# Eight PSUM tiles of one bank in the place of four of two banks

## The chip, the cores and the metric

The kernel runs on one core of a Trainium2 chip. The metric is the device time of one execution in microseconds, taken as the median of several runs.

TensorE (PE) multiplies and writes PSUM, an accumulator memory that this kernel uses as eight banks of 2 KB in each partition. VectorE (DVE) and ScalarE (ACT) read PSUM; GpSimd (POOL) here works on SBUF only; SyncE (SP) issues most of the DMAs. The engines run side by side, each through its own instructions in order, and wait for one another by semaphores.

## The reference

Attention, a gated projection, and a feed-forward block with layer norm, one after another (batch 4, 448 positions, 12 heads of 64, so 1792 rows of 768):

```python
def _moe_ref(x, w_val, conv_w, w_out):
    ...
    gate = 1.0 / (1.0 + np.exp(-gate_pre))      # gate_pre: causal convolution of x, 5 taps
    val = x @ w_val
    return (gate * val @ w_out).astype(np.float32)

def _moe2_ref(x, g_ln, w_ch1, w_ch2):
    mu = np.mean(x, axis=-1, keepdims=True)
    var = np.mean((x - mu) ** 2, axis=-1, keepdims=True)
    xn = (x - mu) / np.sqrt(var + 1e-06) * g_ln
    ch = np.maximum(xn @ w_ch1, 0.0) @ w_ch2     # 768 -> 3072 -> 768
    return (x + ch).astype(np.float32)

def reference(**kwargs):
    attn_out = _attn_ref(**attn_kwargs)          # causal softmax attention
    x = ...                                      # heads side by side
    x = _moe_ref(x=x, **moe_kwargs)
    return _moe2_ref(x=x, **moe2_kwargs)
```

## The kernel before

The attention and the gate fill the first 254.9 us; the change doesn't touch them. Behind them come three stages of matmuls.

The **w_out stage** (254.9 to 356.9 us). `tile_steps(n)` handles 128 rows, for 14 tiles. TensorE multiplies gate * val by w_out (L812, 36 matmuls of 384 columns), the two halves of the 768 columns into the two banks of one PSUM tile (tag "o": `Z[0]` and `Z[1]` in turn). VectorE takes the statistics of each half (`bn_stats`, L827) and their sums (L835, L836), POOL the power (L839), VectorE the shift (L840). ACT copies the tile for the residual (`ka`, L830) and writes the normalised tile to SBUF (`kn`, L842), in one instruction each for both banks. TensorE transposes it in six blocks (`kt`, L848) into another PSUM tile (tag "x": `Z[3]` and `Z[2]` in turn), and VectorE scales it by g_ln into SBUF (`fx`, L851), again in one instruction. `right_blocks` then makes seven operands of each two tiles: additions (`tt`, L712) and a split of each operand into a high (ACT, L866) and a low part (DVE, L867).

The **W1 stage** (356.9 to 684.7 us), `unit1`. The product with w_ch1 is computed by a scheme of seven block products; each product runs for two groups of rows (512 and 384 columns wide), in six visits of the weights. One unit is one product of one group: nine matmuls (L1038) into one bank, 168 units in all. The sums of products are made partly by accumulating in a bank and partly by emptying it: ACT copies the first results to SBUF (L1050), VectorE adds later ones to the copies (L1053), ACT applies the relu (L1009), and ACT issues the store to DRAM (L1014). Meanwhile ACT and DVE prepare the weights of the coming visits from DRAM (L264 to L283, L751, L753, additions L712), and parts of them are stored by SP (L975).

The **W2 stage** (684.7 to 1001.7 us), `unit`. The same scheme for w_ch2: 196 units of nine matmuls of 384 columns (L1154). VectorE alone empties the banks, by an addition to a sum in SBUF (L1165); ACT and DVE make both operands (L1136, L1137, L1098, L1099).

The eight banks in W1 and W2 are three rings, by the letter that the unit's number in "ACABACA" has (`MINE` in W2):

```python
Z = [ps.tile([P, 2, 512], F32, name=f"z{i}") for i in range(4)]
"A": [Z[3][:, 0], Z[0][:, 0], Z[1][:, 0], Z[2][:, 0]], "C": [Z[3][:, 1], Z[1][:, 1]], "B": [Z[0][:, 1], Z[2][:, 1]],
```

So neighbouring banks of one tile serve different rings. The planner knows banks: `Plan.ready` asks whether the users of the same place of the ring are done. The waits in the program itself are made afterwards by the tile framework, from the tile that an instruction reads or writes (`reuse_waits="tile"` of the pool `ps`).

What sets the order: all of this is handed to `Plan` as steps, `task(cost, fn, due, ...)`, each with an engine (or several), a cost in ns and a due time. `arrange()` goes through time and gives each free engine the ready step with the earliest due time; the instructions of each engine are written in that order. `TUNE` shifts the due times by kind of step, and `HOME` says for some additions whether POOL or VectorE takes them.

Of the kernel before, what the change touches and what calls it, by code (L numbers as in the profile page):

```python
# [52 lines left out]
class Plan:  # L53
# [28 lines left out]
    def task(self, cost, fn, due, after=(), new=(), uses=(), lag=0, mode=None, hog=False, behind=None, key=None):  # L82
        due += self.tune.get(key, 0)
        if key in self.home:
            cost = {self.home[key]: {'POOL': 1040, 'DVE': 554}[self.home[key]]}

        def run():
            for b in new:
                b.tile = self.place(b)
            fn(k.engine)  # L90

        k = Task(cost, run, due, after, new, uses, lag, mode, hog, behind)
        self.tasks.append(k)
        return k
# [91 lines left out]
def attention_gate_ffn(  # L186
# [428 lines left out]
    JJ = 3  # L615
# [12 lines left out]
    with ExitStack() as ph2, tc.manual_schedule():  # L628
# [10 lines left out]
        Z = [ps.tile([P, 2, 512], F32, name=f"z{i}") for i in range(4)]  # L639
# [18 lines left out]
        def raw_view(t):  # L658
# [11 lines left out]
            "o": [Z[0], Z[1]], "x": [flat(Z[i]).rearrange("p (c f) -> p c f", f=P) for i in (3, 2)],  # L670
# [6 lines left out]
            "A": [Z[3][:, 0], Z[0][:, 0], Z[1][:, 0], Z[2][:, 0]], "C": [Z[3][:, 1], Z[1][:, 1]], "B": [Z[0][:, 1], Z[2][:, 1]],  # L677
# [53 lines left out]
        def products_of(who, wa, ws, narrowed, due, out):  # L731
# [7 lines left out]
            k1 = task({"POOL": 1040}, lambda e: tt(e, s(), q(2)(), q(3)(), ALU.add), due + 0.2, narrowed, [ws], [wa], hog=True, key=who + "s1")  # L739
            k3 = task({"POOL": 1040}, lambda e: tt(e, q(2)(), q(0)(), q(2)(), ALU.subtract), due + 0.6, [k1], [], [wa], hog=True, key=who + "s3")  # L740
# [498 lines left out]
```

## Time and profile before

| | us |
| --- | --- |
| median of 3 runs | 1007.7 (1007.18 to 1008.37) |
| profiled execution | 1007.35 |
| its span | 1005.6 |
| TensorE busy | 963.7 |
| VectorE busy | 765.0 |
| ScalarE busy | 561.6 |
| GpSimd busy | 294.5 |
| granted TensorE clock, mean | 0.998 |

The span is the stretch that the profile covers, from the first instruction to the last; 1.75 us of the execution lie outside it. Matmuls overlap one another, so a busy TensorE says little of single stops: these are seen in the chain of waits, which is the row of instructions and releases that ended last, and in the list of what TensorE waited for. In the rows below an instruction reads "line engine operation out<-in", and the names leave the numbers of tiles out: every PSUM tile of these stages is `z`. Where the number matters, the order of the compiled program has it (z0_3198 is `Z[0]`, z3_3201 is `Z[3]`).

### The profile page before, as it was taken

What the parts mean: (1) busy time and instruction counts of PE and PEld (TensorE: products, weight loads), DVE (VectorE), ACT (ScalarE), POOL (GpSimd) and SP (SyncE); (2) the same over time, 40 slices, a digit from 0 to 9 for tenths busy, and PEclk for the clock granted to TensorE, in tenths of its full rate; (3) what the DMA queues carried; (4) which work ended last, traced back from release to release, by engine and by line L of the source; (5) the groups of instructions that cost most, each with busy time, mean ns of one, the idle gap of its engine ahead of it and who ended that gap; (6) DMA issues with size and microseconds to landing.
All of it is one profiled execution on the core that took longest, in us unless ns stands there. A gap on an engine that the chain in (4) does not pass through costs nothing.

```text
span 1005.6 us, 16427 instructions
## 1 busy us (share of the span) xinstructions
PE 963.7 (96%) x5731; PEld 857.0 (85%) x5731; DVE 765.0 (76%) x1549; ACT 561.6 (56%) x1153; POOL 294.5 (29%) x367
## 2 busy tenths in 40 slices
PE   9989999999999989999979999999999999999998
PEld 5657777788999978888868878888999999999998
DVE  6899989864488876666667776667999888979873
ACT  7988878862365556666555556564445335334330
POOL 5888877671032231111111121110110000100100
PEclk9999999999999999999999999999999999999999
DMA  6344445322554467878787877689725424424322
GB/s 199 118 158 146 153 154 164 113 83 87 160 173 143 141 225 249 254 222 264 244 251 250 271 223 237 207 265 321 272 84 179 145 63 157 134 82 147 126 95 95
DMA packets 115474, 177.26 MB, mean 176 GB/s; under 512 B 10432, under 2 KB 87744, under 8 KB 115392
## 3 DMA queue, kind: packets, MB, share of 16 engines
q1 hardware_dynamic: 70704, 154.19, 46.3%
q10 hardware_dynamic: 44688, 22.03, 7.5%
q8 instruction: 45, 0.74, 0.3%
q14 instruction: 37, 0.30, 0.1%
HBM read 118.39 MB, written 57.80 MB: 175 GB/s over the span
## 4 chain that ended last, share of the span: by engine, by line
PE 72%; DVE 14%; POOL 4%; DMA 3%; ACT 3%; issue 3%; SPq 0%; ACTq 0%; DVEq 0%; POOLq 0%
PE z L1154 28%; PE z L1038 24%; PE val L599 5%; PE z L812 5%; PE t L443 2%; PE pv L467 2%; PE s L599 2%; DVE g L485 2%; PE s L372 2%; POOL p L408 2%; DVE p L394 1%; DVE x L867 1%; DVE lf L1053 1%; DMA lf<-in_w_ch 1%; DMA hd<-lf 1%
## 5 line engine op out<-in xcount | busy, mean ns | idle before, releaser
L1038 PE MATMUL z<-x,ar 128*128 128x512 f32 (+1 forms) x1224 | 256.5, 368 | 15.4 <-DVE lf L1053 6.3
L1038 PEld LDWEIGHTS z<-x,ar 128*128 128x128 f32 x1224 | 222.9, 189 | 46.5 <-ACT lf L1050 7.9
L712 POOL TENSOR_TENSOR lf<-lf 128x384 f32<-128x384 f32 x52 | 59.4, 1142 | 332.7 <-DVE lf L712 162.3
L1154 PE MATMUL z<-x,x 128*128 128x384 f32 x684 | 125.4, 335 | 1.8 <-DVE lf L1165 0.8
L1165 DVE TENSOR_TENSOR acc<-z,acc 128x384 f32<-128x384 f32 x168 | 91.6, 552 | 46.6 <-PE z L1154 45.4
L1154 PEld LDWEIGHTS z<-x,x 128*128 128x128 f32 x684 | 118.8, 188 | 3.5 <-issue 1.8
L1136 ACT CAST x<-lf 128x384 fp32r<-128x384 f32 x102 | 51.3, 513 | 87.3 <-PE z L1154 67.2
L812 PE MATMUL z<-wo,ar 128*128 128x384 f32 x504 | 91.2, 337 | 0.4 <-DVE ar L801 0.4
L812 PEld LDWEIGHTS z<-wo,ar 128*128 128x128 f32 x504 | 87.0, 188 | 1.1 <-DVE ar L801 0.9
L1154 PE MATMUL z<-x,ar 128*128 128x384 f32 x468 | 85.4, 334 | 0.4 <-ACT ar L1136 0.4
L408 POOL TENSOR_SCALAR p<-p,r 128x128 f32<-128x128 f32 (+1 forms) x144 | 78.4, 567 | 22.4 <-DVE r L404 21.4
L1154 PEld LDWEIGHTS z<-x,ar 128*128 128x128 f32 x468 | 81.4, 188 | 0.7 <-issue 0.7
L400 ACT ACTIVATE p<-p,negm 128x128 f32<-128x128 f32 (+1 forms) x144 | 71.9, 504 | 12.5 <-DVE negm L394 11.7
L485 DVE SCALAR_TENSOR_TENSOR g<-pv,cw,g 128x444 f32<-128x444 f32 (+1 forms) x96 | 64.7, 674 | 11.0 <-POOL g L476 9.0
L1050 ACT COPY lf<-z 128x512 f32<-128x512 f32 (+1 forms) x72 | 37.6, 535 | 52.7 <-PE z L1038 52.0
L1038 PE MATMUL z<-x,w 128*128 128x512 f32 (+1 forms) x288 | 61.8, 366 | 1.4 <-DVE lf L1053 1.4
L1137 DVE TENSOR_TENSOR x<-lf,x 128x384 fp32r<-128x384 f32 x102 | 59.6, 594 | 3.2 <-DMA af<-wd 1.6
L1009 ACT ACTIVATE lf<-lf 128x512 f32<-128x512 f32 (+1 forms) x72 | 41.6, 577 | 36.4 <-DVE lf L1053 32.8
L1038 PEld LDWEIGHTS z<-x,w 128*128 128x128 f32 x288 | 52.4, 188 | 8.6 <-ACT lf L1009 1.8
L1136 ACT CAST ar<-lf 128x384 fp32r<-128x384 f32 x57 | 28.7, 513 | 52.9 <-PE z L1154 43.6
L1053 DVE TENSOR_TENSOR lf<-z,lf 128x512 f32<-128x512 f32 (+1 forms) x72 | 43.5, 618 | 16.5 <-PE z L1038 15.7
L753 DVE TENSOR_TENSOR ar<-lf,ar 128x384 fp32r<-128x384 f32 x62 | 38.1, 619 | 22.8 <-ACT ar L751 22.2
(152 smaller groups left out, 1855.3 us busy)
## 6 DMA issues: line engine op xcount, KB each, us to landing
lf<-in_w_ch SPq DMA_DIRECT2D x31, 768.0 KB, 5.7
af<-wd SPq DMA_DIRECT2D x28, 576.0 KB, 4.9
lf<-hd SPq DMA_DIRECT2D x19, 768.0 KB, 4.4
raw<-in_qk SPq DMA_DIRECT2D x24, 512.0 KB, 4.6
hd<-lf ACTq DMA_DIRECT2D x48, 256.0 KB, 4.1
af<-in_w_ch SPq DMA_DIRECT2D x15, 768.0 KB, 5.2
wd<-af SPq DMA_DIRECT2D x60, 192.0 KB, 3.2
hd<-lf ACTq DMA_DIRECT2D x48, 192.0 KB, 4.5
```

Of the source, the lines that this page charges most:

```text
L400: nc.scalar.activation(reg, reg, AF.Exp, bias=negm.tile[:, i:i + 1], scale=-1.0, accum_out=ssum.tile[:, i:i + 1])
L408: nc.gpsimd.tensor_scalar(reg, reg, r.tile[:, i:i + 1], 1.0, ALU.mult, ALU.mult)
L485: nc.vector.scalar_tensor_tensor(g.tile[:, d:], pv.tile[:, :S - d], cw[:, c, t:t + 1], g.tile[:, d:], ALU.mult, ALU.add)
L599: nc.tensor.matmul(ps.tile[:, :S], w[:, do, kc * P:(kc + 1) * P], x.tile, start=(kc == 0 and i == 0), stop=(kc == KC - 1 and i == 2),)
L712: ENG[eng].tensor_tensor(o, a, b, op)
L812: nc.tensor.matmul(o.tile[:, nh, :HALF], y.tile[:, kc], wo_t[kc][:, a, nh * HALF:(nh + 1) * HALF], start=(count[nh] == 0), stop=(count[nh] ...
L1038: nc.tensor.matmul(b.tile[:, :width], w.tile[:, a, kc], X[g][p][:, c, kc], start=(m == 0 and fresh), stop=(m == 3 * JJ - 1), skip_group_ch ...
L1053: ka = task({"DVE": 154 + int(1.04 * width)}, lambda e: nc.vector.tensor_tensor(q.tile, b.tile[:, :width], q.tile, ALU.add), t1, [k], [], ...
L1136: k_hi = task({"ACT": 514}, lambda e, src=src, h=h: nc.scalar.copy(h.tile[:, 0], src()), due, [need, k_hi], [h], [buf], key=f"chi{i}")
L1137: k = task({"DVE": 554}, lambda e, src=src, h=h: nc.vector.tensor_tensor(h.tile[:, 1], src(), f32(h.tile[:, 0]), ALU.subtract), due + 1, [ ...
L1154: nc.tensor.matmul(b.tile[:, :HALF], h.tile[:, a, jj], w.tile[:, c, jj], start=(n == 0 and fresh), stop=(n == 3 * JJ - 1), skip_group_chec ...
L1165: k = task({"DVE": 554}, lambda e: nc.vector.tensor_tensor(acc(), b.tile[:, :HALF], acc(), ALU.add), t0 + UNIT + 0.2, [k, acc_ld[u]], [], ...
```

## The change

The four tiles of two banks become eight of one bank. What read or wrote two banks in one instruction (the copy `ka`, the normalising `kn`, the scaling `fx`) is now two instructions, one for each bank, and their costs in the planner are raised, as are those of additions on POOL and of the low parts in W2. `TUNE` and `HOME` have new numbers. In `HOME` es2, Xt3, Xt4, Zt1, Zt2, ws1 and T4 go from POOL to DVE; es4, ws3 and T1 go from DVE to POOL. (X and Z are `right_blocks` of the two groups, ws the additions of a W1 visit, T those of W2's weights, es those of W1's first weights.) In the w_out stage 12 additions L712 go to VectorE, and POOL keeps 2 of 14.

```diff
-TUNE = {'eld': -26.4, 'ea': -8.5, 'eb0': 2.2, ...
-HOME = {'es1': 'DVE', 'es3': 'POOL', 'es2': 'POOL', 'es4': 'DVE', 'Xt1': 'DVE', 'Xt2': 'DVE', 'Xt3': 'POOL', ...
+TUNE = {'eld': -20.7, 'ea': -38.2, 'eb0': 2.2, ...
+HOME = {'es1': 'DVE', 'es3': 'POOL', 'es2': 'DVE', 'es4': 'POOL', 'Xt1': 'DVE', 'Xt2': 'DVE', 'Xt3': 'DVE', ...
...
-            cost = {self.home[key]: {'POOL': 1040, 'DVE': 554}[self.home[key]]}
+            cost = {self.home[key]: {'POOL': 1095, 'DVE': 554}[self.home[key]]}
...
-        Z = [ps.tile([P, 2, 512], F32, name=f"z{i}") for i in range(4)]
+        Z = [[ps.tile([P, 512], F32, name=f"z{i}_{h}") for h in range(2)] for i in range(4)]
...
-            "o": [Z[0], Z[1]], "x": [flat(Z[i]).rearrange("p (c f) -> p c f", f=P) for i in (3, 2)],
+            "o": [Z[0], Z[1]], "x": [Z[3], Z[2]],
...
-            "A": [Z[3][:, 0], Z[0][:, 0], Z[1][:, 0], Z[2][:, 0]], "C": [Z[3][:, 1], Z[1][:, 1]], "B": [Z[0][:, 1], Z[2][:, 1]],
+            "A": [Z[3][0], Z[0][0], Z[1][0], Z[2][0]], "C": [Z[3][1], Z[1][1]], "B": [Z[0][1], Z[2][1]],
...
-            ka = task({"ACT": 800}, lambda e: nc.scalar.copy(stage.tile.rearrange("p (a f) -> p a f", a=2), o.tile[:, :, :HALF]),
+            def kept(e):
+                for nh in range(2):
+                    nc.scalar.copy(stage.tile[:, nh * HALF:(nh + 1) * HALF], o.tile[nh][:, :HALF])
+
+            ka = task({"ACT": 870}, kept,
...
-            kn = task({"ACT": 1000}, lambda e: nc.scalar.activation(
-                xn.tile.rearrange("p (a f) -> p a f", a=2), o.tile[:, :, :HALF], AF.Identity, bias=nm.tile, scale=rs.tile),
-                D(n - 2), [km], [xn], [nm, rs, o], key="kn")
+            def normed(e):
+                for nh in range(2):
+                    nc.scalar.activation(xn.tile[:, nh * HALF:(nh + 1) * HALF], o.tile[nh][:, :HALF], AF.Identity, bias=nm.tile, scale=rs.tile)
+
+            kn = task({"ACT": 1080}, normed, D(n - 2), [km], [xn], [nm, rs, o], key="kn")
...
-                    nc.tensor.transpose(x.tile[:, kc, :], xn.tile[:, kc * P:(kc + 1) * P], ident)
+                    nc.tensor.transpose(x.tile[kc // JJ][:, kc % JJ * P:(kc % JJ + 1) * P], xn.tile[:, kc * P:(kc + 1) * P], ident)
...
-            return task({"DVE": 957}, lambda e: nc.vector.tensor_tensor(
-                fx.tile.rearrange("p q c f -> p (q c) f"), x.tile[:, :KC], g_t[:, :, None].to_broadcast([P, KC, P]), ALU.mult),
-                D(n - 1), [kt_], [fx], [x], key="fx")
+            def scale(e):
+                for q in range(2):
+                    nc.vector.tensor_tensor(fx.tile[:, q], x.tile[q][:, :QU].rearrange("p (c f) -> p c f", f=P),
+                                            g_t[:, q * JJ:(q + 1) * JJ, None].to_broadcast([P, JJ, P]), ALU.mult)
+
+            return task({"DVE": 1024}, scale, D(n - 1), [kt_], [fx], [x], key="fx")
...
-                w_made[kk, i] = task({"DVE": 1260}, lambda e, sg=sg, b=b: nc.vector.tensor_tensor(
+                w_made[kk, i] = task({"DVE": 1350}, lambda e, sg=sg, b=b: nc.vector.tensor_tensor(
```

How the compiled order shows it, on TensorE in the first visit of W1, before; the last two rows are the product that starts at 429.23 us in the trace. In a row, the first name is the tile written, then the weights' and rows' tiles, and behind it the engines waited for.

```order
L1038 MATMUL z0_3198<-x1_2_3790,ar_3180 128x384 x9
L1038 MATMUL z0_3198<-x0_5_3193,ar_3180 128x512 x2
L1038 MATMUL z0_3198<-x0_5_3193,ar_3180 128x512 [waits DVE_49]
L1038 MATMUL z0_3198<-x0_5_3193,ar_3180 128x512 x6
L1038 MATMUL z2_3200<-x1_5_3793,ar_3180 128x384 x9
L1038 MATMUL z3_3201<-x0_3_3191,ar_3180 128x512 [waits Activation_49]
L1038 MATMUL z3_3201<-x0_3_3191,ar_3180 128x512
L1038 MATMUL z3_3201<-x0_3_3191,ar_3180 128x512 [waits DVE_49]
L1038 MATMUL z3_3201<-x0_3_3191,ar_3180 128x512 x6
L1038 MATMUL z0_3198<-x1_3_3791,ar_3180 128x384 [waits DVE_49,Activation_49]
L1038 MATMUL z0_3198<-x1_3_3791,ar_3180 128x384 x8
```

The same units after:

```order
L1047 MATMUL z0_0_3198<-x1_2_3785,ar_3180 128x384 [waits Activation_49]
L1047 MATMUL z0_0_3198<-x1_2_3785,ar_3180 128x384 x8
L1047 MATMUL z0_1_3199<-x0_5_3193,ar_3180 128x512 x2
L1047 MATMUL z0_1_3199<-x0_5_3193,ar_3180 128x512 [waits DVE_49]
L1047 MATMUL z0_1_3199<-x0_5_3193,ar_3180 128x512 x6
L1047 MATMUL z2_1_3203<-x1_5_3788,ar_3180 128x384 x9
L1047 MATMUL z3_0_3204<-x0_3_3191,ar_3180 128x512 [waits Activation_49]
L1047 MATMUL z3_0_3204<-x0_3_3191,ar_3180 128x512
L1047 MATMUL z3_0_3204<-x0_3_3191,ar_3180 128x512 [waits DVE_49]
L1047 MATMUL z3_0_3204<-x0_3_3191,ar_3180 128x512 x6
L1047 MATMUL z0_0_3198<-x1_3_3786,ar_3180 128x384 [waits Activation_49]
L1047 MATMUL z0_0_3198<-x1_3_3786,ar_3180 128x384 x8
```

The units stand in the same order and in the same banks; z0_3198 is now z0_0 and z0_1, and the last unit has only the wait for ACT, which copies z0_0, and none for VectorE, which reads z0_1.

On VectorE at the end of the w_out stage, before: an addition and low parts of operands (L867), the last tile's statistics (L827), and the scaling (L851) of the tile before it out of z3, into whose first bank W1's first unit then writes.

```order
L712 TENSOR_TENSOR af_3181<-af_3181 128x384 [waits DVE_49]
L867 TENSOR_TENSOR x1_1_3789<-af_3181,x1_1_3789 128x3x128 [waits Activation_49]
L867 TENSOR_TENSOR x1_2_3790<-af_3181,x1_2_3790 128x3x128 [waits Activation_49]
L827 BN_STATS st_4177<-z1_3199 128x6 [waits PE_49]
L827 BN_STATS st_4177<-z1_3199 128x6
L835 BN_AGGR mv_4181<-st_4177 128x2 [waits DVE_49]
L836 TENSOR_SCALAR rs_4182<-mv_4181 128x1 [waits DVE_49]
L867 TENSOR_TENSOR x1_4_3792<-af_3181,x1_4_3792 128x3x128 [waits Activation_49]
L867 TENSOR_TENSOR x1_3_3791<-af_3181,x1_3_3791 128x3x128
L840 SCALAR_TENSOR_TENSOR nm_4189<-mv_4181,rs_4182 128x1 [waits Pool_49]
L851 TENSOR_TENSOR af_3181<-z3_3201,g_t_63 128x768 [waits DVE_49,PE_49]
```

The same place after:

```order
L712 TENSOR_TENSOR af_3181<-af_3181 128x384
L876 TENSOR_TENSOR x1_2_3785<-af_3181,x1_2_3785 128x3x128 [waits Activation_49]
L876 TENSOR_TENSOR x1_3_3786<-af_3181,x1_3_3786 128x3x128 [waits Activation_49]
L876 TENSOR_TENSOR x1_4_3787<-af_3181,x1_4_3787 128x3x128 [waits Activation_49]
L876 TENSOR_TENSOR x1_1_3784<-af_3181,x1_1_3784 128x3x128
L827 BN_STATS st_4214<-z1_0_3200 128x6 [waits PE_49]
L827 BN_STATS st_4214<-z1_1_3201 128x6 [waits PE_49]
L839 BN_AGGR mv_4226<-st_4214 128x2 [waits DVE_49]
L840 TENSOR_SCALAR rs_4227<-mv_4226 128x1 [waits DVE_49]
L859 TENSOR_TENSOR af_3181<-z3_0_3204,g_t_63 128x384 [waits PE_49]
L859 TENSOR_TENSOR af_3181<-z3_1_3205,g_t_63 128x384 [waits PE_49]
L844 SCALAR_TENSOR_TENSOR nm_4233<-mv_4226,rs_4227 128x1 [waits Pool_49]
```

Two low parts have moved ahead of the last statistics, the shift (L840, now L844) behind the scaling, and the scaling is two rows of 384 elements, one for each tile of one bank.

## Rows read from the trace of the kernel before

**Rows 1.** The page: the chain that ended last, shares by line.

```profile
PE z L1154 28%; PE z L1038 24%; PE val L599 5%; PE z L812 5%; PE t L443 2%; PE pv L467 2%; PE s L599 2%; DVE g L485 2%; PE s L372 2%; POOL p L408 2%; DVE p L394 1%; DVE x L867 1%; DVE lf L1053 1%; DMA lf<-in_w_ch 1%; DMA hd<-lf 1%
```

**Rows 2.** Busy time by stretch: stretch, length, engines (instructions), PEclk, DMA share, GB/s.

```profile
290.00:330.00 40.00, 39.61 (x240) 38.86 (x239) 34.51 (x74) 23.86 (x41) 10.74 (x12) 1.00 0.49 159
...
685.00:770.00 85.00, 82.29 (x469) 80.54 (x467) 78.80 (x145) 39.18 (x72) 10.11 (x9) 1.00 0.65 219
```

**Rows 3.** The chain in order of time: start, length, engine, line, instructions.

```profile
356.90 2.34 PE z L1038 x9
359.92 4.39 PE z L1038 x18
...
429.23 53.13 PE z L1038 x260
...
684.84 3.14 PE z L1154 x18
...
880.71 87.66 PE z L1154 x503
968.95 33.04 PE z L1154 x189
```

**Rows 4.** TensorE's waits, 354 to 1006: sum, times, longest (us).

```profile
PE z L1038 <- DVE lf L1053: 7.8, 6, 1.8
PE z L1038 <- ACT lf L1050: 6.1, 3, 4.5
PE z L1154 <- DVE acc L1165: 4.4, 5, 1.5
PE z L1038 <- DVE af L851: 2.9, 1, 2.9
PE z L1154 <- DVE lf L1165: 1.8, 3, 0.8
```

**Rows 5.** TensorE's waits, 255 to 357, one of them.

```profile
PE z L848 <- ACT af L842: 1.4, 1, 1.4
```

**Rows 6.** Timelines of ACT and DVE, 422 to 431: start, length, instruction.

```profile
423.82 0.48 ACT L1050 COPY lf<-z 128x384 f32<-128x384 f32 x1 [3.08 <-PE z L1038]
...
427.93 1.15 DVE L1053 TENSOR_TENSOR lf<-z,lf 128x384 f32<-128x384 f32 x2
```

**Rows 7.** Timelines of ACT and PE around the longest stop.

```profile
521.11 0.60 ACT L1009 ACTIVATE lf<-z 128x512 f32<-128x512 f32 x1 [3.75 <-DMA wd<-lf]
...
525.28 0.57 ACT L1050 COPY lf<-z 128x512 f32<-128x512 f32 x1
...
517.62 3.83 PE L1038 MATMUL z<-x,ar 128*128 128x512 f32 x18
525.91 5.32 PE L1038 MATMUL z<-x,ar 128*128 128x512 f32 x17 [4.45 <-ACT lf L1050]
```

**Rows 8.** Timeline of DVE at the end of the w_out stage.

```profile
353.39 1.03 DVE L827 BATCH_NORM_STATS2 st<-z 128x6 f32<-128x384 f32 x2 [0.22 <-PE z L812]
...
354.77 1.02 DVE L867 TENSOR_TENSOR x<-af,x 128x384 fp32r<-128x384 f32 x2
...
355.89 0.96 DVE L851 TENSOR_TENSOR af<-z,g_t 128x768 f32<-128x768 f32 x1
```

**Rows 9.** Groups by line, 255 to 357: busy us, mean ns, idle before.

```profile
L842 ACT ACTIVATE af<-z,nm,rs 128x768 f32<-128x768 f32 x14 | 13.9, 992 | 9.3 <-DVE nm L840 9.3
...
L851 DVE TENSOR_TENSOR af<-z,g_t 128x768 f32<-128x768 f32 x13 | 12.4, 951 | 0.2
...
L712 DVE TENSOR_TENSOR af<-af 128x384 f32<-128x384 f32 x12 | 7.4, 616 | 0.4
```

**Rows 10.** Timelines of ACT and PE: one tile's normalising and transposes.

```profile
336.90 0.99 ACT L842 ACTIVATE af<-z,nm,rs 128x768 f32<-128x768 f32 x1
...
339.36 0.82 PE L848 MATMUL z<-ident,af 128*128 128x128 f32 x6
```

**Rows 11.** Waits of SP's queue, 480 to 530: sum, times, longest (us).

```profile
SPq L975 <- DVE af L276: 26.0, 4, 10.1
```

More of the change, by code (lines that the diff above doesn't have):

```diff
@@ L32 @@
+HOME = {'es1': 'DVE', 'es3': 'POOL', 'es2': 'DVE', 'es4': 'POOL', 'Xt1': 'DVE', 'Xt2': 'DVE', 'Xt3': 'DVE', 'Xt4': 'DVE', 'Zt1': 'DVE', 'Zt2': 'DVE', 'Zt3': 'POOL', 'Zt4': 'DVE', 'ws1': 'DVE', 'ws3': 'POOL', 'ws2': 'POOL', 'ws4': 'POOL', 'T3': 'DVE', 'T1': 'POOL', 'T2': 'DVE', 'T4': 'DVE', 'sm0': 'DVE', 'sm1': 'POOL', 'sm2': 'DVE', 'sm3': 'DVE'}
 class Buf:
@@ L737, in s @@
                 return ws.tile
-            k1 = task({"POOL": 1040}, lambda e: tt(e, s(), q(2)(), q(3)(), ALU.add), due + 0.2, narrowed, [ws], [wa], hog=True, key=who + "s1")
-            k3 = task({"POOL": 1040}, lambda e: tt(e, q(2)(), q(0)(), q(2)(), ALU.subtract), due + 0.6, [k1], [], [wa], hog=True, key=who + "s3")
+            k1 = task({"POOL": 1095}, lambda e: tt(e, s(), q(2)(), q(3)(), ALU.add), due + 0.2, narrowed, [ws], [wa], hog=True, key=who + "s1")
+            k3 = task({"POOL": 1095}, lambda e: tt(e, q(2)(), q(0)(), q(2)(), ALU.subtract), due + 0.6, [k1], [], [wa], hog=True, key=who + "s3")
             srcs = [(q(0), narrowed[:1], wa), (s, [k1], ws), (s, None, ws), (q(1), narrowed[:1], wa), (q(2), [k3], wa), (s, None, ws),
@@ L745, in products_of @@
                 if i == 2:
-                    need = [task({"POOL": 1040}, lambda e: tt(e, s(), s(), q(0)(), ALU.subtract), due + 0.8, [lo[1]], [], [ws, wa], hog=True, key=who + "s2")]
+                    need = [task({"POOL": 1095}, lambda e: tt(e, s(), s(), q(0)(), ALU.subtract), due + 0.8, [lo[1]], [], [ws, wa], hog=True, key=who + "s2")]
                 if i == 5:
-                    need = [task({"POOL": 1040}, lambda e: tt(e, s(), q(1)(), s(), ALU.subtract), due + 1.2, [lo[2]], [], [ws, wa], hog=True, key=who + "s4")]
+                    need = [task({"POOL": 1095}, lambda e: tt(e, s(), q(1)(), s(), ALU.subtract), due + 1.2, [lo[2]], [], [ws, wa], hog=True, key=who + "s4")]
                 h = out(i)
@@ L812, in products @@
                     nc.tensor.matmul(
-                        o.tile[:, nh, :HALF], y.tile[:, kc], wo_t[kc][:, a, nh * HALF:(nh + 1) * HALF],
+                        o.tile[nh][:, :HALF], y.tile[:, kc], wo_t[kc][:, a, nh * HALF:(nh + 1) * HALF],
                         start=(count[nh] == 0), stop=(count[nh] == 3 * KC - 1),
@@ L873, in right_blocks @@
             l5 = split(5, b21, [ka], a, D(n + 2.3) - 5.5)
[L874 removed]
+            t1 = task({"POOL": 1095}, lambda e: tt(e, b12(), b12(), b11(), ALU.subtract), due, [ka, kb], [], [a, b], hog=True, key=who + "t1")
             l6 = split(6, b22, [kb], b, due + 0.1)
             split(1, b12, [t1], b, due + 0.2)
[L877 removed]
+            t2 = task({"POOL": 1095}, lambda e: tt(e, b22(), b22(), b12(), ALU.subtract), due + 0.3, [t1, l6], [], [b], hog=True, key=who + "t2")
             split(2, b22, [t2], b, due + 0.4)
[L879 to L880 removed]
+            t3 = task({"POOL": 1095}, lambda e: tt(e, b11(), b22(), b11(), ALU.subtract), due + 0.5, [t2, l0], [], [a, b], hog=True, key=who + "t3")
+            t4 = task({"POOL": 1095}, lambda e: tt(e, b21(), b21(), b22(), ALU.subtract), due + 0.6, [t2, l5], [], [a, b], hog=True, key=who + "t4")
             split(3, b11, [t3], a, due + 0.7)
@@ L1120, in chain_steps @@
             for i, (o, a, b, op) in enumerate(sums):
-                k = task({"DVE": 554} if i < 2 else {"POOL": 1040}, lambda e, o=o, a=a, b=b, op=op: tt(e, s.tile[:, o], a(), b(), op), due - 19 + i, [ld, k],
+                k = task({"DVE": 554} if i < 2 else {"POOL": 1095}, lambda e, o=o, a=a, b=b, op=op: tt(e, s.tile[:, o], a(), b(), op), due - 19 + i, [ld, k],
                          [] if i else [s], [r, s] if i else [r], hog=True, key=f"sm{i}")
```

9 lines of the change are left out of this document (2 added, 7 removed).

## The prediction

> **What bounds the kernel now.** I read the shares of the chain first, then the stretches, then the chain in order of time, and only then the waits. The chain runs mostly through the matmuls of the two last stages, L1038 and L1154 [rows 1]. Until 254.9 us, in the attention and the gate, the change touches no instruction, so I leave that part as it is. Behind it TensorE is nearly always busy (39.61 of 40 us in the w_out stage, 82.29 of 85 at the start of the W2 stage [rows 2]), and what is left to win is the sum of its short stops.
>
> Chain pieces without a stop give a matmul's price: 53.13 / 260 = 0.2043 us in the W1 stage, where half have 512 columns and half 384, and 87.66 / 503 = 0.1743 us in the W2 stage [rows 3]. W1 lasts from 356.90 to 684.84, 327.94 us; 1512 x 0.2043 = 308.9; the six transposes between two pieces take 0.84 (359.08 to 359.92), so 18.2 us are stops. W2 ends at 968.95 + 33.04 = 1001.99 and lasts 317.15; 1764 x 0.1743 = 307.5, so 9.7 us are stops. Before W1's first matmul TensorE stands 2.9 us, and once 1.4 us in the w_out stage [rows 4, 5]. In all about 32 us.
>
> What is waited for? The waits name the instructions that empty PSUM: L1053 six times, L1050 three times, L1165 [rows 4]. No maker of weights (L751, L753) is in that list for L1038. The trace leaves tile numbers out, so I put the compiled order beside it. At 429.23 [rows 3] TensorE opens a product in bank 0 of z0. That bank was copied out by ACT from 423.82 to 424.30. The wait is for the second of two VectorE additions (427.93 to 429.08), which reads bank 1 of z0 [rows 6]. The longest stop is alike: the product at 525.91 goes to bank 1 of z3 and waits for ACT's copy of bank 0 (525.28 to 525.85) [rows 7]. The waits are kept for each tile, not for each bank. In the compiled orders 69 of 98 L1038 matmuls that wait for an emptying wait for the neighbour's bank, and 63 of 99 in L1154; in the changed order none does. Following every stop of W1 and W2 over 0.2 us to the read it waited for, I find the other bank each time but once (0.3 us at 692).
>
> **The change, part by part.**
> *W1 (-16.2 us).* The order of units on TensorE stays; their false waits go. What is late next is the bank's own emptying, which mostly has three units of other banks in front of it: from 424.30 to 429.23 in the example, 4.9 us. The stop at 525.91 shrinks rather than vanishes: ACT had stood 3.75 us for a store [rows 7] and copies bank 0 late, while TensorE can now run the product that waited and the next one, 18 matmuls or 3.7 us; of 4.45 us about 0.8 is left. Behind that stop 17 matmuls took 5.32 us where 18 had taken 3.83 before it [rows 7], about 1.7 us more that followed the pause; I credit all but 0.5 of them. With 0.7 for copies that are late elsewhere, 2.0 us stay of 18.2. Bounds: nothing stays, or half stays (9.1) if the retuned preparation turns out to be as tight as the banks were.
>
> *W2 (-8.0 us).* Same mechanism, 9.7 us. VectorE empties every bank here and also makes W2's operands, and it is busy 78.80 of 85 us at the start [rows 2]; once already a product waited for data there and not for a bank (the 0.3 us). I leave 1.7 us standing; bounds 0 and 5.
>
> *The step from w_out to W1 (-0.9 us).* The first product needs bank 0 of z3, which L851 reads until 356.85. Before it VectorE runs the last statistics from 353.39, two L867 in 1.02, L840, then L851 [rows 8]. Now the scaling is two instructions, only the first of which the product waits for (about 0.45 us sooner), and no L867 stands between. Against that 7.0 us of VectorE work now stand between the last two statistics, where a tile lasts 6.9, so they may start up to 1 us late. Gain 0.4 to 1.4; I take the middle.
>
> *The w_out stage (+0.6 us).* Three instructions on two banks become six on one. Their price: the pair of L867 with 384 columns takes 1.02 us and the pair of L1053 out of PSUM, one of them 512 wide, 1.15, against 0.951 for L851 over 768 [rows 6, 8, 9], so 0.07 to 0.20 us a tile on VectorE, and at 14 tiles 1 to 2.8 us. ACT's L842 (0.992 us) and L830 pay about the same; ACT has the room. Of the table HOME, 12 additions L712 come from POOL to VectorE (616 ns each [rows 9]), 7.4 us more for VectorE in the stage. The path to be kept is statistics, L842, transposes: L842 ends at 337.89 and the transposes start at 339.36 [rows 10], so 1.5 us cover it. One or two moved additions ahead of the statistics (0.6 or 1.2 us) fit; three overrun by 0.4. I take 1.0 us for overruns, with bounds 0 and 4, less 0.4 of the 1.4 us stop of L848, which now needs only the first half of L842.
>
> [...]
>
> *Other moves.* In W1 the steps ws1 and T4 go to VectorE, ws3 and T1 to POOL: about even. VectorE itself loses idle time, since its reads no longer wait for later products in the neighbour's bank. I count neither.
>
> **The sum.** -16.2 - 8.0 - 0.9 + 0.6 = -24.5 us. The profiled execution took 1007.35 us (span 1005.6, 1.75 around it), so 982.9; the median lies 0.35 us above the profiled execution, hence 983.2, stated as 983.
>
> **The rivals.**
> *A. Half the gain.* Behind the false waits stands the preparation: weights from DMA through ACT and VectorE, and VectorE in the w_out stage, at 34.51 of 40 us from 290 to 330 [rows 2]; with (7.4 + 1.9) x 40 / 99 = 3.8 us more it would be at 38.3 of 40. For it: TensorE asks for everything 5% sooner. Against it: no wait of L1038 names a maker of weights. With 9 us of W1's and 4 of W2's stops left and w_out at +4: -9.1 - 5.7 - 0.4 + 3.6 = -11.6, about 996.
>
> *B. No gain.* The trace shows the release that came last, so beneath the neighbour's wait another could lie close by: the bank's own emptying, because the same VectorE and ACT empty all banks and are late with all. Then the split only renames the wait: about 1007, with 0 to -2 us. Against it are the 4.9 us of the example. [...]
>
> *C. Slower: the order of SP's queue.* Weights and intermediate results share SP's queue, and a store whose data is late holds every load behind it: L975 waited for VectorE 26.0 us in four times between 480 and 530, the longest 10.1 [rows 11], and TensorE's list shows no wait from that. The new due times place these stores and their makers anew (T4 moves to VectorE, T1 to POOL). If a hold came to exceed the lead of the loads by 6 us in each of the five later visits of W1, 30 us would be lost against 24.5 won: 1013. It decides from 5 us of excess a visit; before, the excess is nil with holds of 10.
>
> **Chances.** Main case (977 to 989) 0.70; A (989 to 1000) 0.18; B (1005.7 to 1009.7) 0.04; C 0.05; more than forecast, below 977, 0.03 (all stops gone would be 1007.7 - 32 = 975.5). The range goes from 976 to 996: the main case and most of A, about 0.83. A measurement of this kernel tells about 0.2%, 2 us, from no change. Faster 0.92, the same 0.03, slower 0.05.
>
> **What would show it.** In the trace after, TensorE's waits for L1050, L1053 and L1165 (the same operations under new line numbers) should fall from 20 us to under 4, and W1 should last about 312 us, W2 about 309. The w_out stage should keep its length within 2 us, with the split instructions at 0.5 us each, and the stop ahead of W1 should be about 2 us. I am wrong if those waits stay with the bank's own read as releaser (B), if waits for L751, L753, L1137 or a DMA take their place (A, C), if transposes wait for L842 tile after tile, or if W1's matmuls run at a lower granted clock than now.

## The result

The changed kernel takes 975.31 us (median; 975.01 to 975.59) against 1007.44 us before on the same chip: a ratio of 0.968, 95% interval 0.9663 to 0.9697. The forecast was 983 with a range from 976 to 996. The direction and the mechanism came as forecast; the gain is 32.1 us instead of 24.5, and the time lies 0.7 us below the range. The profiled execution took 975.12 us, its span is 973.3.

The page of the kernel after: span, busy time, the chain by line (what answers to [rows 1]).

```profile
span 973.3 us, 16474 instructions
...
PE 953.6 (98%) x5731; PEld 857.0 (88%) x5731; DVE 778.9 (80%) x1577; ACT 564.7 (58%) x1181; POOL 280.5 (29%) x353
...
PE z L1047 32%; PE z L1163 31%; DVE x L876 0%; DVE x L1146 0%; DVE st L827 0%; DVE af L712 0%; DVE acc L1174 0%; DVE af L859 0%; DVE x L1108 0%; DVE lf L1174 0%; DVE ar L801 0%; DVE ar L1146 0%; ACT ar L236 0%; PE z L854 0%; ACT af L848 0%
```

The lines have moved. L1047 and L1163 are the matmuls L1038 and L1154 of before, L1059 and L1062 the copy L1050 and the addition L1053 of W1, L1018 its relu (L1009), L1174 the addition L1165 of W2, L1145 and L1146 its operands (L1136, L1137). In the w_out stage L848 is the normalising (L842), L854 the transposes (L848), L859 the scaling (L851), L875 and L876 the two parts of the operands (L866, L867).

The two matmul lines carry 63% of the chain instead of 52%, and no DMA and no emptying of a bank stands in it with more than a fraction of a per cent. The chain in order of time, as in [rows 3], shows how unbroken it is (start, length, engine, line, instructions):

```profile
354.82 2.34 PE z L1047 x9
357.16 0.65 PE z L854 x6
357.81 305.73 PE z L1047 x1503
663.55 4.69 PE z L1163 x27
...
676.20 293.57 PE z L1163 x1692
```

W1 runs through 1503 matmuls in one piece. (From 668 to 676 us the chain goes by VectorE, while TensorE works on without a stop.) TensorE's complete list of waits from 250 us to the end, for [rows 4 and 5], has three entries:

```profile
PE z L1047 <- DVE af L859: 2.7, 1, 2.7
PE z L854 <- ACT af L848: 1.1, 1, 1.1
PE z L812 <- ACT ar L236: 0.2, 1, 0.2
```

The 20 us of waits for L1050, L1053 and L1165 are gone to the last one. Busy time by stretch (columns as in [rows 2]):

```profile
290.00:330.00 40.00, 40.00 (x243) 39.83 (x242) 36.58 (x84) 25.54 (x53) 4.33 (x7) 1.00 0.51 169
...
450.00:530.00 80.00, 80.00 (x395) 71.36 (x394) 60.79 (x90) 49.79 (x85) 15.19 (x13) 1.00 0.85 275
...
664.00:749.00 85.00, 84.86 (x490) 84.57 (x489) 82.12 (x152) 41.13 (x74) 11.77 (x10) 1.00 0.65 224
```

The last one is, as in [rows 2], the first 85 us of W2, which now begins at 663.55. TensorE is busy nearly all the time in each; VectorE has risen to 36.58 of 40 us in the w_out stage and 82.12 of 85 at W2's start, and still TensorE has no wait for it there.

By stage, from the first matmul of one line to that of the next:

| stage | before | after | difference | forecast |
| --- | --- | --- | --- | --- |
| up to the first L812 | 255.13 | 253.85 | -1.3 | 0 |
| L812 to W1's first matmul | 101.77 | 100.97 | -0.8 | -0.3 |
| W1 | 327.94 | 308.73 | -19.2 | -16.2 |
| W2 to its last matmul | 317.15 | 306.22 | -10.9 | -8.0 |
| sum | | | -32.2 | -24.5 |

### The profile page after: what moved, and what is told of

Its sections match the earlier page's. It is cut to its first block, busy times and chain, and to the rows that moved or that the text cites. A ratio compares the mean times of both kernels' runs of the same rounds, so it can differ in the third digit from the quotient of the medians.

```text
span 973.3 us, 16474 instructions
## 1 busy us (share of the span) xinstructions
PE 953.6 (98%) x5731; PEld 857.0 (88%) x5731; DVE 778.9 (80%) x1577; ACT 564.7 (58%) x1181; POOL 280.5 (29%) x353
## 4 chain that ended last, share of the span: by engine, by line
PE 62%; DVE 2%; ACT 0%; issue 0%; DVEq 0%
PE z L1047 32%; PE z L1163 31%; DVE x L876 0%; DVE x L1146 0%; DVE st L827 0%; DVE af L712 0%; DVE acc L1174 0%; DVE af L859 0%; DVE x L1108 0%; DVE lf L1174 0%; DVE ar L801 0%; DVE ar L1146 0%; ACT ar L236 0%; PE z L854 0%; ACT af L848 0%
## 5 line engine op out<-in xcount | busy, mean ns | idle before, releaser
L1047 PE MATMUL z<-x,ar 128*128 128x512 f32 (+1 forms) x1224 | 252.2, 365 | 2.7 <-DVE af L859 2.7
L1047 PEld LDWEIGHTS z<-x,ar 128*128 128x128 f32 x1224 | 222.7, 188 | 29.4 <-DVE af L859 2.9
L712 POOL TENSOR_TENSOR lf<-lf 128x384 f32<-128x384 f32 x52 | 62.0, 1193 | 322.4 <-DVE lf L712 274.0
L1163 PE MATMUL z<-x,x 128*128 128x384 f32 x684 | 124.0, 334 | 0.0
L1174 DVE TENSOR_TENSOR acc<-z,acc 128x384 f32<-128x384 f32 x168 | 91.8, 553 | 34.9 <-PE z L1163 31.2
L1163 PEld LDWEIGHTS z<-x,x 128*128 128x128 f32 x684 | 119.1, 188 | 0.0
L1145 ACT CAST x<-lf 128x384 fp32r<-128x384 f32 x102 | 51.3, 513 | 87.2 <-PE z L1163 67.8
L812 PE MATMUL z<-wo,ar 128*128 128x384 f32 x504 | 90.8, 337 | 0.2 <-ACT ar L236 0.2
L812 PEld LDWEIGHTS z<-wo,ar 128*128 128x128 f32 x504 | 87.1, 188 | 0.4 <-ACT ar L236 0.4
L1163 PE MATMUL z<-x,ar 128*128 128x384 f32 x468 | 85.2, 334 | 0.1
L1163 PEld LDWEIGHTS z<-x,ar 128*128 128x128 f32 x468 | 81.4, 188 | 0.4 <-issue 0.4
L485 DVE SCALAR_TENSOR_TENSOR g<-pv,cw,g 128x444 f32<-128x444 f32 (+1 forms) x96 | 64.7, 674 | 10.9 <-POOL g L476 9.0
L1146 DVE TENSOR_TENSOR x<-lf,x 128x384 fp32r<-128x384 f32 x102 | 60.3, 604 | 1.5 <-ACT x L1145 1.5
L753 DVE TENSOR_TENSOR ar<-lf,ar 128x384 fp32r<-128x384 f32 x62 | 35.9, 584 | 31.9 <-ACT ar L751 31.7
L1047 PE MATMUL z<-x,w 128*128 128x512 f32 (+1 forms) x288 | 61.2, 365 | 0.0
L1145 ACT CAST ar<-lf 128x384 fp32r<-128x384 f32 x57 | 28.8, 514 | 51.2 <-PE z L1163 48.8
L1018 ACT ACTIVATE lf<-lf 128x512 f32<-128x512 f32 (+1 forms) x72 | 41.1, 576 | 29.9 <-DVE lf L1062 22.5
L1059 ACT COPY lf<-z 128x512 f32<-128x512 f32 (+1 forms) x72 | 38.1, 533 | 35.0 <-PE z L1047 33.4
L1047 PEld LDWEIGHTS z<-x,w 128*128 128x128 f32 x288 | 52.6, 188 | 6.3
L394 DVE CUSTOM_DVE_ANT_0 p<-s,mask 128x128 f32<-128x128 f32 (+1 forms) x144 | 51.9, 417 | 2.5 <-PE s L372 2.4
```

Source lines behind the costliest of these rows:

```text
L394: nc.vector.tensor_tensor_reduce(buf.tile[:, o:o + w], bank.tile[:, at:at + w], m, NEG_SCALE, 3.0e38, ALU.add, ALU.min, negm.tile[:, i:i + 1])
L485: nc.vector.scalar_tensor_tensor(g.tile[:, d:], pv.tile[:, :S - d], cw[:, c, t:t + 1], g.tile[:, d:], ALU.mult, ALU.add)
L712: ENG[eng].tensor_tensor(o, a, b, op)
L812: nc.tensor.matmul(o.tile[nh][:, :HALF], y.tile[:, kc], wo_t[kc][:, a, nh * HALF:(nh + 1) * HALF], start=(count[nh] == 0), stop=(count[nh] ...
L1018: k = task({"ACT": 190 + int(0.84 * n)}, lambda e: nc.scalar.activation(p.tile, src(), AF.Relu), due, [k], [p] if bufs else [], [*bufs] if ...
L1047: nc.tensor.matmul(b.tile[:, :width], w.tile[:, a, kc], X[g][p][:, c, kc], start=(m == 0 and fresh), stop=(m == 3 * JJ - 1), skip_group_ch ...
```

## The experiments

The times of before beside the runs are medians on the chip of the run; they lie between 1007.3 and 1008.0, so the runs of different chips are set side by side here.

**The split alone.** The tiles and the three steps of the change, with `TUNE`, `HOME` and the planner costs of before:

```diff
-            cost = {self.home[key]: {'POOL': 1095, 'DVE': 554}[self.home[key]]}   # and TUNE, HOME,
-            ka = task({"ACT": 870}, kept,                                         # kn, fx, wlo alike
+            cost = {self.home[key]: {'POOL': 1040, 'DVE': 554}[self.home[key]]}
+            ka = task({"ACT": 800}, kept,
```

> The kernel after with the due times, homes and planner costs of before: only the tiles and the three steps are split. Theory 1 (the neighbour's waits were everything; behind them nothing is tight): 975 to 978 us, W1 about 308.7 us and W2 about 306.2 us as in the kernel after, no wait for L1059, L1062 or L1174. Theory 2 (the split leaves the rest that the prediction kept, 2.0 us in W1, 1.7 us in W2 and an overrun in the w_out stage, and the new table took those away): 980 to 984 us, with the late copy near 525 us and the data waits near 692 us still in the list. Theory 3 (the new table is worth much by itself): above 985 us.

Measured: 979.97 us (977.9 to 981.84), ratio 0.9728 (0.9702 to 0.9753). So 27.4 of the 32.1 us are the split; the new table adds 4.7 on top of it. The profiled execution is the longest of the four, 981.84 us, at the lowest mean granted clock (0.997). In it W2 is as fast as in the kernel after (306.2 us), W1 takes 315.0 instead of 308.7. The waits of TensorE from 354 us on:

```profile
PE z L1047 <- ACT ar L751: 2.7, 1, 2.7
PE z L1047 <- DVE af L859: 2.3, 1, 2.3
```

ACT's timeline ahead of the first of them:

```profile
515.43 0.60 ACT L1018 ACTIVATE lf<-z 128x512 f32<-128x512 f32 x1 [4.92 <-DMA wd<-lf]
...
517.45 0.51 ACT L751 CAST ar<-lf 128x384 fp32r<-128x384 f32 x1 [0.44 <-ACT lf L1018]
```

TensorE's timeline behind both:

```profile
355.32 3.79 PE L1047 MATMUL z<-x,ar 128*128 128x512 f32 x9 [2.32 <-DVE af L859]
...
518.01 5.62 PE L1047 MATMUL z<-x,ar 128*128 128x512 f32 x18 [2.72 <-ACT ar L751]
```

And two stretches there (columns as above; the granted clock is the third number from the end):

```profile
356.00:359.00 3.00, 3.00 (x9) 2.22 (x8) 1.03 (x2) 0.90 (x3) 0.00 (x0) 0.50 0.99 383
...
520.00:523.00 3.00, 3.00 (x10) 2.77 (x9) 3.00 (x4) 3.00 (x8) 1.65 (x1) 0.50 0.61 192
```

One stop is left in W1, and it is for weights, not for a bank. ACT stands 4.92 us at 510 us, because a store of W2's weights (DMA wd<-lf) still reads a buffer that ACT's next relu writes; the cast of W1's next weights (L751) is queued behind, and TensorE stops 2.72 us. Behind this stop, and behind the one ahead of W1, the granted clock is 0.50 for some 3 us: nine matmuls take 3.79 us where the kernel after needs 2.34. The stop of 2.7 us and the slow matmuls behind both stops make nearly all of the 6.3 us between the two W1 stages. The shortest of the four executions, at a mean granted clock of 1.000, took 977.90 us: 2.6 us more than the kernel after, about the one stop. The rest of the 4.7 goes with the clock (0.998 in the two middle executions).

**The table alone.** The reverse: two-bank tiles and undivided steps, with `TUNE`, `HOME` and costs of after.

```diff
-TUNE = {'eld': -26.4, 'ea': -8.5, ...
+TUNE = {'eld': -20.7, 'ea': -38.2, ...       # HOME and the costs as in the change
```

> The kernel before, two-bank tiles and steps that read two banks, with the due times, homes and planner costs of the kernel after. Theories 1 and 2: the waits for the neighbour's bank are all back, so 1003 to 1012 us; the order only shifts which of them are long. Theory 3: 995 us or less.

Measured: 1005.29 us, ratio 0.9975 (0.9961 to 0.9988), 2.1 us less than before. TensorE's waits:

```profile
PE z L1038 <- ACT lf L1050: 8.8, 8, 2.4
PE z L1038 <- DVE lf L1053: 6.9, 5, 2.4
```

They sum to no less than before (15.7 against 13.9 us in [rows 4]); all of TensorE's waits from 250 us on sum to 24.1 against 25.6. The mean granted clock differs too, 0.998 in the middle of these ten executions and 0.995 in the middle of the nineteen of before, so what makes the 2.1 us isn't separated here. The order hardly matters as long as the neighbour's bank is waited for.

**The divided instructions alone.** The kernel before, its table and its tiles, with the copy, normalising and scaling as two instructions.

```diff
-            ka = task({"ACT": 800}, lambda e: nc.scalar.copy(stage.tile.rearrange("p (a f) -> p a f", a=2), o.tile[:, :, :HALF]),
+            def kept(e):
+                for nh in range(2):
+                    nc.scalar.copy(stage.tile[:, nh * HALF:(nh + 1) * HALF], o.tile[:, nh, :HALF])
+            ka = task({"ACT": 800}, kept,                 # kn and fx alike
```

> The kernel before with its own table and its two-bank tiles, but the copy, the normalising and the scaling of the w_out stage written as two instructions for each tile (42 more instructions). If the price is what the rows say, 0.07 to 0.20 us a tile on VectorE and ACT beside TensorE's work: 1007 to 1008.5 us, no difference. If each of them lies on the path: 1010 to 1013 us.

Measured: 1008.67 us, ratio 1.0017 (1.0004 to 1.0031): 1.3 us more (0.4 to 3.1), 0.2 us above the 1007 to 1008.5 expected of a price beside TensorE's work, and below the 1010 to 1013 of one on the path. From its first matmul to the last transposes that stand ahead of W1, the w_out stage took 98.7 us against 98.1. The scaling, by group:

```profile
L859 DVE TENSOR_TENSOR af<-z,g_t 128x384 f32<-128x384 f32 x26 | 13.2, 549 | 0.2
```

Two of 549 ns against one of 951 in [rows 9]; started back to back, a pair of such halves takes 1.01 to 1.02 us in the timeline. On VectorE the price is the lower end of what the rows said, 0.06 to 0.07 us a tile. ACT pays more than "about the same": two halves of the normalising take 1.23 us in the timeline of the kernel after (at 342.55 us) against 0.99 for the whole in [rows 10], but TensorE doesn't wait longer for it (1.1 us in all, against 1.4 in [rows 5]).

**Half of the tiles split.** The split with the old table, but z0 and z2 stay one tile of two banks, used through their halves.

```diff
-        Z = [[ps.tile([P, 512], F32, name=f"z{i}_{h}") for h in range(2)] for i in range(4)]
...
+            if i in (0, 2):
+                pair = ps.tile([P, 2, 512], F32, name=f"z{i}")
+                Z.append([pair[:, 0], pair[:, 1]])
...
```

> The split with the old table, but only two of the four tiles are split: z1 and z3 into single banks, z0 and z2 still one tile of two banks (used through their halves; the order of the instructions is that of the full split). If the neighbour's waits are the cause, what comes back is the sum of the stops of the kernel before that were for z0 (8.0 us in W1) and z2 (1.4 in W1, 2.6 in W2): 12 us over the full split's 980.0, so 989 to 994 us, with the stops for z0 back. If the two-instruction steps or the order made the gain: 979 to 982 us.

Measured: 991.74 us, ratio 0.9838 (0.9823 to 0.9852), where the sum of the stops for z0 and z2 gave 992. TensorE's waits (here the copy is L1065, the additions are L1068 and L1180, L757 is L751 and L865 the scaling):

```profile
PE z L1053 <- DVE lf L1068: 6.5, 4, 1.8
PE z L1053 <- DVE af L865: 2.5, 1, 2.5
PE z L1053 <- ACT ar L757: 2.3, 1, 2.3
PE z L1053 <- ACT lf L1065: 1.5, 1, 1.5
PE z L1169 <- DVE acc L1180: 1.3, 2, 0.7
PE z L1169 <- DVE lf L1180: 0.5, 1, 0.5
```

The order of the instructions is that of the full split; only the waits differ. This shows the mechanism without the table and without the divided steps. The waits for an emptying that are back sum to 9.8 us, not to the 12 that were forecast, so that the times agree within 0.3 us is in part luck.

**What the new table repaired.** Five runs put parts of the new `TUNE` and `HOME` on the split, each with the planner costs of before; "the search" in their expectations is the making of the new table. First the steps that make W2's weights, whose stores held ACT at 510 us (in `TUNE` r2, u0, u1, T1 to T4 and wd0 to wd6, in `HOME` T1 and T4):

> The split with the old table (980.0 us), but the due times and homes of one group of steps from the new table: the making of W2's weights (r2, u0, u1, T1 to T4, wd0 to wd6). In the split with the old table ACT stood 4.9 us at 510 us for a store of those weights to leave a buffer that the next relu wants, the cast of W1's weights came late behind it, TensorE stopped 2.7 us at 515 and then ran 3 us at half the clock. Theory 1 (that one queue of ACT is what the search repaired): the stop goes, 975.5 to 977.5 us. Theory 2 (the repair lies in other steps): the stop stays, 979 to 981 us.

Measured: 981.0 us (979.96 to 981.93), no gain over the split alone. W1 is as short as in the kernel after, but W2 begins with a new stop. VectorE's timeline there:

```profile
677.73 0.56 DVE L1174 TENSOR_TENSOR lf<-z,lf 128x384 f32<-128x384 f32 x1
678.20 1.55 DVE L1108 TENSOR_TENSOR x<-af,x 128x1152 fp32r<-128x1152 f32 x1
679.68 1.01 DVE L1174 TENSOR_TENSOR acc<-z,acc 128x384 f32<-128x384 f32 x2
```

TensorE's:

```profile
680.84 5.48 PE L1163 MATMUL z<-x,ar 128*128 128x384 f32 x21 [3.15 <-DVE acc L1174]
```

VectorE's instructions follow one another without a gap that the timeline would mark, and the addition that frees the wanted bank is late in its queue. With the split alone W1 ended 5.5 us later and no such stop is in the list; that the stop in W1 gave VectorE the time for W2's start fits this, but no run shows it by itself.

Then all steps that serve W2, with the stage's own (the same, and accld, sgld, whi, wlo, rld, sm, chi, clo and ac):

> The split with the old table, but the new due times and homes of all steps that serve W2: the making of its weights (as in the run with 981.0 us, where the stop at 515 us went and one of 3.1 us came at W2's start, for an addition late in VectorE's queue) and the steps of the W2 stage itself. If these two groups are what the search repaired: both stops are gone, 975 to 977 us. If the stop at W2's start comes from W1's steps (VectorE comes to W2 late because W1 ends sooner): it stays, 979 to 982 us.

Measured: 980.62 us (978.7 to 982.64). W1 is whole again, and the stop at W2's start stays, 2.8 us for L1174, so W2's steps alone don't remove it. The complement, W2's steps old and all others new:

> The complement: the split with the new due times and homes of the w_out stage and of W1's steps, and the old ones of all that serves W2. If the search's gain lies in W2's steps: the stop near 515 us for L751 is there, 979 to 986 us. If it lies in W1's own steps: 975 to 977 us.

Measured: 985.17 us, ratio 0.978 (0.976 to 0.98), with the wait for L751 (1.8 us) and five others in W1 and W2. And by kind of number, first the new homes alone, then the new due times alone:

> The split with the old due times and planner costs, and the new homes (which additions go to POOL and which to VectorE). Theory 1 (the homes of T1 and T4 repair the stop at 515 us): 975 to 977.5 us. Theory 2 (it takes the due times): 979 to 983 us, the stop still there, and the 12 additions that VectorE takes over in the w_out stage show as a stop or not at all.

> The split with the new due times, but the old homes and planner costs. Theory 1 (homes repair it): 979 to 983 us. Theory 2 (due times repair it): 975 to 977.5 us.

Measured: 985.06 us and 985.54 us, both slower than the split with the old table, both with a longer stop for L751 (3.3 and 4.5 us). Neither theory holds. No half of the due times and homes, cut in either way, brings the last 4.7 us; only the whole table does. The planner costs were old in all five runs, and new due times and homes with old costs weren't run, so which of its numbers are needed stays open, and whether the costs are among them.

**Ahead of W1.** The 2.7 us stop is the longest that is left. First both rings are renamed so that W1's first two products go to z0:

```diff
-            "A": [Z[3][0], Z[0][0], Z[1][0], Z[2][0]], "C": [Z[3][1], Z[1][1]], "B": [Z[0][1], Z[2][1]],
+            "A": [Z[0][0], Z[3][0], Z[1][0], Z[2][0]], "C": [Z[0][1], Z[1][1]], "B": [Z[3][1], Z[2][1]],
...
```

> The kernel after with the rings of banks renamed, so that W1's first two products go to the banks of z0, free since the normalising of the last tile but one, and not to those of z3, which VectorE still scales. If the 2.7 us stop ahead of W1 is that bank alone: it goes, 972.3 to 973 us. If the operand or the weights come just behind it (their load is due 10 us ahead): 973 to 975 us with a wait for a DMA or for L876. If the last tile's transposes, now two products later, are late for their readers: 975 us or more.

Measured: 977.68 us (977.14 to 978.98), slower than the kernel after in each of its four executions. W1 opens without a stop, and two others stand a little later (TensorE's timeline):

```profile
351.95 4.39 PE L1047 MATMUL z<-x,ar 128*128 128x512 f32 x18
...
361.18 5.44 PE L1047 MATMUL z<-x,ar 128*128 128x512 f32 x27 [1.36 <-DVE af L712]
368.52 1.66 PE L1047 MATMUL z<-x,ar 128*128 128x384 f32 x8 [1.90 <-ACT lf L1059]
```

The rings serve W1 and W2 to their ends, so the renaming changes more than the opening: two stops are new in W2 as well, 1.1 us for L1146 and 1.0 for L1174.

Then only the A ring:

```diff
-            "A": [Z[3][0], Z[0][0], ...
+            "A": [Z[0][0], Z[3][0], ...
...
```

> The kernel after with only the A ring renamed (z0's first bank before z3's), so W1's first product need not wait for the scaling, the second one still does, and the transposes of the last tile stay behind the first two products. If the stop ahead of W1 is that one bank: 2.7 us shrink to about 1.3, 973.5 to 974.5 us. If the stop only hides the operands of the last tiles, as the renaming of both rings showed (977.7 us, with waits for L712 and L1059 in its place): 975 to 978 us, with a wait behind the last transposes.

Measured: 977.22 us (974.59 to 977.73). TensorE's waits:

```profile
PE z L1047 <- DMA ar<-w1d: 1.4, 1, 1.4
PE z L854 <- ACT af L848: 1.2, 1, 1.2
...
PE z L1047 <- DVE af L859: 0.2, 1, 0.2
```

One stretch:

```profile
270.00:274.00 4.00, 4.00 (x14) 4.00 (x15) 3.90 (x10) 2.51 (x5) 0.55 (x1) 0.57 0.79 283
```

The bank's stop (L859) has shrunk to 0.2 us, and a load of W1's weights takes its place. The profiled execution, the longest of its four, has besides a stretch at a clock of 0.57 behind the stop for L848 at the start of the w_out stage, which the renaming doesn't touch. No version here beats the kernel after by its median; the shortest execution of this one, 974.59 us, is 0.4 us below its shortest.

## Why the prediction was right and wrong

**The mechanism is shown.** The waits were for the neighbour's bank: they vanish with the split (0 of 20 us), come back with two-bank tiles under the new table, and come back in part when half of the tiles span two banks, with a time (991.7) near the one summed from the trace of before (992).

**The step that failed** is the new table, counted at nothing. "The order of units on TensorE stays" holds, but the order on the other engines doesn't, and of their moves the prediction says "I count neither". It gave the table room only as a danger (half of W1's stops staying, rival C). Measured: the split with the old table takes 979.97 us, inside the range; the table's 4.7 us more take the time to 975.31, below it. The two large terms of the split itself are mis-sized too, in opposite directions, so that they nearly cancel: W1 13.0 us in place of 16.2, W2 11.0 in place of 8.0.

**W1, -16.2 forecast, -19.2 measured.** Two errors of opposite sign stand in this term. For the order that I had traced it was too high: the split alone gives 327.94 - 314.98 = 13.0 us in its profiled execution, two stretches at half the clock included. What misled here is "No maker of weights (L751, L753) is in that list": the list names the release that came last, and in the longest stop the weights lay beneath the bank. The trace of before had it. The cast of weights by ACT that TensorE waits for in the split alone has its counterpart at 523.20 us, 1.7 us after TensorE had stopped (525.91 - 4.45 = 521.46), and was hidden by the copy at 525.28 [rows 7]. ACT's timeline before:

```profile
523.20 0.51 ACT L751 CAST ar<-lf 128x384 fp32r<-128x384 f32 x1 [0.44 <-ACT lf L1009]
```

So of 4.45 us 2.7 were left in the split alone, not 0.8, and the clock's fall behind it, to 0.50, came with them; I had credited "all but 0.5" of the slow matmuls without looking at the clock. Rival B warns of another wait close beneath, but means the bank's own emptying; a wait for L751 is the sign that the prediction gives for rival A, and A is right at this one place. The table then took both away, and that is the second error, the one above: between the two profiled executions it is worth 6.3 us in W1.

**W2, -8.0 forecast, -10.9 measured.** The mis-sized term is the 1.7 us that I left standing because VectorE was busy 78.80 of 85 us. The split alone has no stop of TensorE there, neither for a bank nor for the two waits of 0.4 us for L1136, a maker of operands, that TensorE's list of before holds at 880.70 and 968.95 us and [rows 4] leaves out. VectorE had been kept waiting by the same tiles, which the prediction names ("VectorE itself loses idle time") and counts at nothing. Its waits for a product ahead of W2's additions, before, with half of the tiles split, and with all split, at the same table:

```profile
DVE acc L1165 <- PE z L1154: 45.4, 53, 2.6
DVE acc L1180 <- PE z L1169: 39.0, 50, 2.6
DVE acc L1174 <- PE z L1163: 35.0, 62, 1.0
```

Its busy 93% was no sign that it was the limit; in the kernel after it is busy 97% of the same stretch without a stop of TensorE.

**The price of a matmul.** The pieces that I took as free of stops (0.2043 and 0.1743 us) were not quite: in the kernel after they are 305.73 / 1503 = 0.2034 and 293.57 / 1692 = 0.1735. Over 1512 and 1764 matmuls that is 1.4 us each, by which the sums of stops, 18.2 and 9.7, were too low. It is also why 975.5, the time with "all stops gone", was no floor: the kernel after lies 0.2 us below it with stops of 2.7 and 1.1 us left.

**Ahead of W1, -0.9 forecast, -0.2 measured (2.9 to 2.7 us).** VectorE came to the last statistics 1.5 us after the transposes had begun, against 0.2 us before (353.39 [rows 8] and 353.19): 1.3 us later, where I had allowed up to 1. Its row in the kernel after:

```profile
352.85 1.02 DVE L827 BATCH_NORM_STATS2 st<-z 128x6 f32<-128x384 f32 x2
```

The transposes on TensorE:

```profile
351.34 0.82 PE L854 MATMUL z<-ident,af 128*128 128x128 f32 x6
```

In the split with the old table the stop is 2.3 us. The two renamings show that taking the bank's wait away gains little by itself: in them waits for the weights' load and for the last operands stand behind it.

**The w_out stage, +0.6 forecast, -0.6 measured.** Nothing overran. The divided steps by themselves cost 0.6 us of the stage (third run, 98.7 against 98.1), as forecast. With the tiles split as well it is 97.9, and with the moved additions of the new table 97.5, so no cost of these shows on the path; what they cost VectorE is below.

**Before L812** 1.3 us lie in a part that the change leaves alone. Among the kernels here its end varies from 253.6 to 255.1 us, and both ends have the old table, so this much of the gain of the profiled execution looks like chance.

**The range.** The bounds of the terms sum to 29.7 us, a time of 978.0, and "all stops gone" gave 975.5; I gave all below 977 a chance of 0.03, since I held a residue in every stage for likely. The residues of the split alone were single places, not a share of each stage, and the new table removed the one in W1. With the table counted at nothing there was no case for this side. In the kernel after rivals A and C didn't come: no wait for weights, operands or DMA in W1 or W2, at a DMA share of 0.85 in place of 0.79 from 450 to 530 us.

## What to carry to other kernels

Compare what a wait is recorded for with what is really read and written: with waits kept by tile, a tile that spans two banks made the users of one bank wait for the other here, writers (20 us of TensorE's waits, gone with the split) and readers (45.4 us of VectorE's waits ahead of W2's additions, 35.0 with the split) alike, and the divided instructions cost 1.3 us by themselves, on engines that had room. A list of waits shows the last release alone; before a wait is removed, look up when the next input of the same instruction was ready. Removing stops also moves the load of the next stage forward (W2 began with a stop of 3.15 us in the run whose W1 ended 5.5 us sooner), so an order of steps that was good with the stops may have to be made anew, and a change that comes with new due times needs a term for them.

## What the runs showed of the hardware

Short stops cost more than their length in some executions: nine matmuls behind a stop of 2.3 us took 3.79 us in the split alone, against 2.34 in the kernel after. Behind stops of 2.3 and 2.7 us the split alone shows a granted clock of 0.50 for some 3 us; a renamed version has 0.57 over 4 us behind a stop of 1.2 us, and the kernel before 0.50 behind the stop that began at 521 us:

```profile
527.00:529.00 2.00, 2.00 (x7) 1.52 (x6) 2.00 (x3) 1.29 (x3) 1.60 (x1) 0.50 0.61 198
```

The kernel after has a stop of 2.7 us and no such stretch in its profile (9 matmuls in 2.34 us). What decides between the two was not found; the split alone varies by 3.9 us over its four executions, from 977.90 us at a mean granted clock of 1.000 to 981.84 at 0.997, the kernel after by 0.6, all at 1.000.

A mean can hide one long instruction. The prediction took 616 ns, the mean of [rows 9], for each addition L712 that moves to VectorE. Shortest, middle and longest (ns) in the w_out stage, before and after:

```profile
L712 DVE TENSOR_TENSOR af<-af x12: 557/558/1261, 280.1 to 350.9; 128x384 f32<-128x384 f32 x12
L712 DVE TENSOR_TENSOR af<-af x24: 550/555/560, 278.3 to 350.5; 128x384 f32<-128x384 f32 x24
```

The one of 1261 ns ran beside an addition of POOL's; the timelines of both engines:

```profile
281.19 1.27 POOL L712 TENSOR_TENSOR early_f<-early_f 128x384 f32<-128x384 f32 x1 [1.60 <-DVE early_r L753]
281.62 1.26 DVE L712 TENSOR_TENSOR af<-af 128x384 f32<-128x384 f32 x1
```

The low parts (L867) show the same: their middle is 551 ns before and after, and their mean fell from 587 to 552, mostly since three of 1.02 us are gone, each of which ran beside additions of POOL's. Beside POOL's short L839 they took 0.55 to 0.62 us. In the kernel after POOL keeps only 2 of the 14 additions. VectorE's load from 290 to 330 us rose by 2.1 us, where I had counted 3.8.
